# A gated linear-attention and bilinear-GLU kernel: another seven-product scheme for gate/up and q, seven products for 17 of 18 output row pairs, and an instruction order taken from a list scheduler inside the program

## The chip, the cores and the metric

The kernel runs on one core of one Trainium2 chip. The metric is the device time of one execution in microseconds (us), smaller is better. The kernel before took 592.59 us, the median of three runs (590.53 to 592.73).

## The reference, cut to what matters

`x` is 2048 x 512. Two branches read it and are mixed by a gate of each token:

```
qkv = x @ wqkv                       # 512 -> 3*512, 32 heads of 16
pq, pk = phi(q), phi(k)              # phi(t) = (t > 0 ? t + 1 : exp(t)) + 1e-6
kv = einsum("bhsd,bhse->bhde", pk, v);  z = sum_s pk
a  = (pq @ kv) / (pq @ z + 1e-6) @ wo
b  = ((x @ w_gate) * (x @ w_up)) @ w_down      # F = 1792
g  = sigmoid(sum(x * gate_w))
out = g * a + (1 - g) * b
```

Everything is float32. The kernel writes each factor as a rounded high part plus a rest and makes each product with three matmuls: high by high, high by low, low by high.

## The kernel before, in words

**First phase** (source lines 212 to 388). For 16 token tiles TensorE makes k = x wk (12 matmuls, `k_mm`) and adds phi(k)^T x to four accumulators (12 matmuls, `g_unit`). Beside it ScalarE and VectorE split the operands, and from step 6 on (`plan`) they prepare the sums of x blocks and of weights for the second phase.

**Second phase, units.** The tokens are halved into two `pair`s of 2 x 512 tokens. In each pair 14 column blocks of gate and up (`f`) and 2 of q (`q`) are made by 16 **units**, 32 in all (`unit`, L493). A unit is a 2 x 2 block product by seven products instead of eight; each product is 2 x 3 = 6 matmuls of 128 x 512 into one of four PSUM banks Y, X, R, S. Between products, ScalarE and VectorE move or add banks (`m2`, `t`, `cross`), and at the end VectorE multiplies gate by up.

**Weights of a unit.** Seven sums of weight blocks stand in a buffer `wr` (two buffers). `w_load` (L166) brings three blocks in one DMA on SyncE's queue; `w_add` (L173) makes two ScalarE copies and one accumulating DMA of 640 KB on GpSimd's queue; `w_high` and `w_low` split the seven sums into `wch` and `wcl` (two buffers each).

**Second phase, output jobs.** The outputs are sums over 18 rows of weights per pair (14 of w_down, 4 of the attention's folded `wp`), taken two rows at a time: nine row pairs per pair of tokens, 18 in all. Six of the 18 are **plain**: eight jobs (one for each 128 x 512 block of output) of two rows x 3 matmuls (`down_jobs`, L739), into `pdn`. Twelve go by **seven products** (`seven`, L792): seven steps, each of 2 x 3 matmuls for a row pair, two row pairs to a group, accumulated in `sa` and `sb`. Their operands are sums of `cross` tiles (split into `xh`, `xl`) and sums of weight rows (`ws`, split into `wh`, `wl`).

**Order.** Nothing is reordered behind the program's back: every engine runs its instructions in the order in which the code emits them. Which job goes between which products of a unit stands in the tables `FIRST` and `SECOND`, when a group opens in `FIRST_AT` and `STARTS`, and how far ahead ScalarE, VectorE and the loads may work in `LEAD_X`, `LEAD_W`, `MOST` and others (lines 32 to 59). The last thing computed is a plain row pair.

Helpers record most instructions, so the profile's lines are those of helpers: L79 matmul, L85 ScalarE, L88 and L91 VectorE, L109 a DMA from SyncE, L112 an accumulating DMA from GpSimd.

Of the kernel before, what the change touches and what calls it, by code (L numbers as in the profile page):

```python
# [14 lines left out]
P = 128  # L15
S = 2048
# [15 lines left out]
LEAD_X = 4  # L32
LEAD_W = 17
GAP_L = 6
GAP_A = 14
HB = 8
FIRST_SEVEN = (((4, 5), (6, 7)), (('a', 0), (8, 9)))
FIRST_AT = (4, 8)
MINUS_AT = (1, 2, 3)
XAT = (11, 6, 4, 8, 11, 7, 11, 13, 13, 13, 10, 13)  # L40
WUNIT = (8, 5, 2)
FIRST = (
    (3, 1, 3, 0), (0, 3, 2, 1), (0, 0, 1, 1), (2, 0, 1, 0), (0, 1, 0, 2), (0, 0, 0, 1), (1, 2, 0, 2), (0, 3, 0, 0),
    (0, 0, 2, 2), (0, 2, 3, 1), (2, 1, 1, 1), (3, 2, 0, 2), (2, 0, 1, 0), (3, 3, 3, 3), (1, 2, 0, 0), (3, 0, 2, 3),
)
PLACES = "high low e m c d t s r end".split()
ATT = ((0, 8, 5, 4, 6, 4, 5, 3), (0, 5, 12, 5, 0, 9, 4, 13))
NS = 58
SECOND = (
    (2, 1, 1, 0), (0, 0, 1, 3), (2, 1, 0, 3), (1, 0, 0, 0), (0, 1, 0, 2), (0, 0, 1, 2), (2, 0, 0, 2), (0, 2, 0, 1),  # L50
    (0, 2, 1, 2), (2, 2, 2, 0), (0, 0, 2, 1), (0, 3, 3, 1), (0, 3, 1, 0), (2, 2, 0, 1), (3, 0, 2, 3), (3, 1, 0, 2),
)
STARTS = (0, 4, 4, 10)
MOST = (2, 2, 2, 2)
MOST_0 = (1, 1, 2, 2)
LEAD_X0 = 4
LEADS_0 = (15, 7, 12)
RELOAD = ((0, 1), (0, 2), (3, 4), (5, 6))
Q_AFTER = ((5, 9), (0, 3))

SLOT = {3: 0, 4: 1, 2: 2, 5: 3, 1: 4, 6: 5, 7: 6}
# [3 lines left out]
def gated_mix(ctx: ExitStack, tc, xt, xp, x, wqkv, wq, wq_add, wo, wgu, wgu_add, wdn, gate_w, out):  # L71
# [39 lines left out]
    def dma_add(dst, src):  # L111
# [17 lines left out]
    own = {i: [const.tile([P, 2, CH], F32R, name=f"xc{i}{v}") for v in "hl"] for i in (1, 4, 6)}  # L129
    xc = {2: [v[:, 0:2] for v in xa], 7: [v[:, 2:4] for v in xa],  # L130
          3: [v[:, 0:2] for v in xb], 5: [v[:, 2:4] for v in xb], **own}


    zeros = own[1][0][:, 0, 0:CH // 2].bitcast(mybir.dt.bfloat16)
# [9 lines left out]
    xsum = {i: dram.tile([P, 2, CH], F32, name=f"xsum{i}") for i in (1, 5, 6, 7)}  # L144
# [28 lines left out]
    def w_add(n):  # L173

        if n < len(order):
            _, kind, m = order[n]
# [4 lines left out]
    PARTS = ((0, 2), (2, 4), (4, 7))  # L181
# [7 lines left out]
    def w_low(n, part):  # L189
        if n < len(order):  # L190
# [5 lines left out]
    SUMS = {1: (A1, B2, 0), 3: (B1, B2, 1), 4: (A2, A1, 1), 6: (A1, B1, 0), 7: (A2, B2, 0), 2: (None, A1, 0),  # L196
            5: (None, B2, 0)}

    def x_load(tile_, pair, i, ks):
        dma(tile_, xp[pair, SUMS[i][1]][:, ks])  # L200

    def x_add(tile_, pair, i, ks):
        one, _, sub = SUMS[i]
        if sub:
            act(tile_, tile_, scale=-1.0)
        if one is not None:
            dma_add(tile_, xp[pair, one][:, ks])
# [4 lines left out]
    with tc.tile_pool(name="p1", bufs=2, reuse_waits="tile") as p1:  # L212
# [127 lines left out]
        def cb_load(i):  # L340
            cbs[i] = p1.tile([P, 2, CH], F32, tag="cbs", name="cbs", bufs=3)
            x_load(cbs[i], 0, i, slice(0, 2))

        for t, i in zip((6, 7, 9, 10, 12), (4, 1, 6, 7, 3)):
            plan(t, lambda i=i: cb_load(i))
            plan(t + 2, lambda i=i: x_add(cbs[i], 0, i, slice(0, 2)))
            plan(t + 5, lambda i=i: split(*xc[i], cbs.pop(i)))
        for n, t in ((0, 8), (1, 11)):
            plan(t, lambda n=n: w_load(n))
            plan(t + 2, lambda n=n: w_add(n))  # L350
        plan(14, lambda: w_high(0))
        for part in range(3):
            plan(14 + part // 2, lambda part=part: w_low(0, part))
        plan(16, lambda: w_load(2))
# [36 lines left out]
    p2 = ctx.enter_context(tc.tile_pool(name="p2", bufs=1, reuse_waits="tile"))  # L391
    live = []
    spare, kept = [], {}

    class Buf:

        def __init__(self, name, rounded=False):
            self.home = rounded and bool(spare)
            one = spare.pop(0) if self.home else p2.tile([P, CH], F32R if rounded else F32, tag="s", name=name, bufs=NS)
            self.f = one.bitcast(F32) if rounded else one  # L400
            self.r = one
            if not self.home:
                live.append(self)
                assert len(live) <= NS, clock[0]

    def put(*some):
        for one in some:
            if one.home:
                spare.append(one.r)
            else:  # L410
                live.remove(one)

    def two(name):
        return [Buf(name + v, True) for v in "hl"]

    def split_buf(name, src, copy="act"):

        hi, lo = two(name)
        split(hi.r, lo.r, src, copy)
        return hi, lo  # L420


    at = {}

    def later(n, place, fn):
        at.setdefault((n, place), []).append(fn)

    def do(n, place):
        for fn in at.pop((n, place), []):
            fn()  # L430
        clock[0] += 1
        most = MOST if n >= units else MOST_0
        advance(dve=most[0], act=most[1])


    jobs, clock = [], [0]

    class Job:

        def __init__(self, mms, chains=(), after=None, apart=0, group=None, first=False):  # L440
            self.first, self.mms, self.after, self.apart, self.group = first, mms, after, apart, group
            self.chains = [list(c) for c in chains]
            self.free = [0] * len(self.chains)

    def always():
        return True

    def advance(**most):

        for i, job in enumerate(jobs):  # L450
            for k, chain in enumerate(job.chains):
                while chain:
                    kind, lead, gap, fn, ready = chain[0]
                    if lead < i or clock[0] < job.free[k] or not ready() or not most.get(kind, 1):
                        break
                    if kind in most:
                        most[kind] -= 1
                    fn()
                    job.free[k] = clock[0] + gap
                    chain.pop(0)  # L460

    owed, passed, running = [0], [0, 0], [None]

    def down(k, all_=False):

        owed[0] += k
        for _ in range(owed[0]):
            if not jobs or passed[0] - passed[1] < jobs[0].apart and not all_:
                break
            waits = [stage for chain in jobs[0].chains for stage in chain]  # L470
            if waits and not all_:
                break
            for kind, lead, gap, fn, ready in waits:
                assert ready(), clock
                fn()
            job = jobs.pop(0)
            running[0] = job.group
            owed[0] -= 1
            clock[0] += 1
            job.mms()  # L480
            passed[1] = passed[0]
            most = MOST_0 if job.first else MOST
            advance(dve=most[2], act=most[3])
            if job.after:
                job.after()
        if not jobs:
            owed[0] = 0


    def share(n):  # L490
        return SECOND[n - units] if n >= units else FIRST[n]

    def unit(n, quad=None, sign=None, og=None):  # L493

        wh, wl = wcs.pop(n)
        bank = {t: psum.tile([P, CH], F32, tag=t, name=f"b{t}") for t in "YXRS"}

        def reload(i):
            if n + 1 == units and i not in xsum:
                spare.extend(v[:, k] for v in xc[i] for k in range(2))  # L500
            elif n + 1 == units:
                hi, lo = xc[i]
                dma(lo.bitcast(F32), xsum[i])

                def high():
                    act(hi, lo.bitcast(F32))

                def low():
                    tt(lo, lo.bitcast(F32), hi.bitcast(F32), ALU.subtract)

                places, use = RELOAD[(1, 5, 6, 7).index(i)], {1: "d", 5: "t", 6: "s", 7: "r"}[i]
                assert places[0] <= places[1] <= PLACES.index(use)
                for fn, at_ in zip((high, low), places):
                    m, one = divmod(at_, len(PLACES))
                    later(units + m, PLACES[one], fn)

        def product(i, to, start=False):
            for k in range(2):
                ks = slice(k * P, (k + 1) * P)
# [25 lines left out]
        if n:  # L545
            w_high(n + 1)
# [4 lines left out]
        if n:  # L551
            w_low(n + 1, 0)
# [694 lines left out]
```

## Time and profile before

| | us |
|---|---|
| median of three runs | 592.59 |
| lowest, highest | 590.53, 592.73 |
| span of the profiled execution | 591.5 |
| TensorE (PE) busy | 583.7 |
| TensorE weight loads (PEld) busy | 478.0 |
| VectorE (DVE) busy | 491.3 |
| ScalarE (ACT) busy | 364.9 |
| GpSimd (POOL) busy | 100.3 |

The span runs from the first to the last instruction of one profiled execution. No whole time is listed for that execution; its span lies 1.1 us under the median of the runs. In the profile an arrow `out<-in` names the tile written and the tiles read. PE is a matmul, PEld its weight load (it runs beside the matmul before). A matmul's shown duration is longer than the distance to the next one, since matmuls are pipelined; so distances between starts are read, not durations.

### The profile page before, as it was taken

The numbers are of one execution on the slowest core, as the hardware profiler recorded it, in microseconds if no ns is written. First come the engines' busy times: TensorE is split into PE (matmuls) and PEld (weight loads), VectorE is DVE, ScalarE is ACT, GpSimd is POOL, SyncE is SP. The second block draws the span as 40 slices with busy tenths as digits, with TensorE's granted clock in tenths as the row PEclk, the third lists the DMA queues.
The fourth block names the chain that finished last, engine by engine and source line by source line (L and its number), as shares of the span: only waits on it lengthen the run. The fifth ranks groups of instructions, "written<-read, shape, count | busy, mean of one in ns | idle before, by whom it ended". The sixth has DMA issues, their size and how long they took to land.

```text
span 591.5 us, 7915 instructions
## 1 busy us (share of the span) xinstructions
PE 583.7 (99%) x2610; PEld 478.0 (81%) x2610; DVE 491.3 (83%) x798; ACT 364.9 (62%) x649; POOL 100.3 (17%) x123
## 2 busy tenths in 40 slices
PE   9999999999999999999999999999999999999997
PEld 6888888888888868788888788888888888888886
DVE  6877895775567889999869967998798999799987
ACT  3856774677647475688456747458956846646520
POOL 0011100000151124111020042305010322301000
PEclk9999999999999999999999999999999999999999
DMA  9476946868898879556798699779875676834003
GB/s 296 168 201 129 284 106 197 213 194 225 252 225 205 204 211 208 146 120 161 213 239 248 211 221 224 226 155 244 215 168 133 176 148 148 186 71 63 0 2 142
DMA packets 68249, 106.19 MB, mean 180 GB/s; under 512 B 8864, under 2 KB 40352, under 8 KB 68192
## 3 DMA queue, kind: packets, MB, share of 16 engines
q1 hardware_dynamic: 51872, 68.98, 35.5%
q0 software_dynamic: 16048, 36.18, 34.9%
q10 hardware_dynamic: 288, 0.52, 0.3%
q8 instruction: 20, 0.33, 0.2%
q14 instruction: 21, 0.17, 0.1%
HBM read 90.70 MB, written 15.61 MB: 180 GB/s over the span
## 4 chain that ended last, share of the span: by engine, by line
PE 90%; DVE 5%; issue 2%; DMA 2%; ACT 1%; POOL 0%; DVEq 0%; POOLq 0%; ACTq 0%
PE bY L79 13%; PE bX L79 13%; PE bR L79 13%; PE sa L79 11%; PE pdn L79 9%; PE sb L79 8%; PE pk L79 8%; PE gt L79 7%; PE bS L79 7%; DMA wr<-in_wgu_add 2%; DVE wcl L88 1%; DVE acc L88 1%; PE warm L79 1%; PE pw L79 0%; DVE cross L88 0%
## 5 line engine op out<-in xcount | busy, mean ns | idle before, releaser
L88 DVE TENSOR_TENSOR wcl<-wr,wch 128x512 fp32r<-128x512 f32 (+1 forms) x96 | 73.2, 772 | 2.0 <-ACT wch L85 1.9
L85 ACT ACTIVATE wch<-wr 128x512 fp32r<-128x512 f32 (+1 forms) x96 | 60.3, 691 | 4.9 <-DMA wr<-in_wgu_add 4.6
L112 POOL DMA_DIRECT2D wr<-in_wgu_add x28 | 25.0, 892 | 207.7 <-ACT wr L85 153.4
L79 PE MATMUL bX<-xbh,wch 128*128 128x512 f32 x128 | 47.3, 390 | 0.0
L79 PE MATMUL bX<-xbl,wch 128*128 128x512 f32 x128 | 47.2, 389 | 0.0
L79 PE MATMUL bX<-xbh,wcl 128*128 128x512 f32 x112 | 43.6, 389 | 0.0
L85 ACT ACTIVATE cross<-bY 128x512 f32<-128x512 f32 x32 | 19.0, 594 | 33.4 <-PE bY L79 33.3
L88 DVE TENSOR_TENSOR bR<-bX,m 128x512 f32<-128x512 f32 x32 | 22.2, 695 | 20.5 <-PE bX L79 19.6
L85 ACT ACTIVATE m<-bY 128x512 f32<-128x512 f32 x32 | 19.0, 593 | 31.7 <-PE bY L79 31.7
L112 POOL DMA_DIRECT2D ws<-dminus x27 | 31.1, 1341 | 35.7 <-DVE wl L88 24.7
L85 ACT ACTIVATE wr<-wr 128x512 f32<-128x512 f32 x64 | 36.4, 618 | 0.3 <-DMA wr<-in_wgu 0.3
L85 ACT ACTIVATE xh<-cross 128x512 fp32r<-128x512 f32 x38 | 23.5, 626 | 20.7 <-DVE cross L88 19.7
L88 DVE TENSOR_TENSOR t<-bR,cross 128x512 f32<-128x512 f32 x32 | 22.0, 687 | 15.0 <-PE bR L79 6.9
L88 DVE TENSOR_TENSOR acc<-pdn,acc 128x512 f32<-128x512 f32 (+1 forms) x39 | 25.4, 671 | 8.1 <-PE pdn L79 7.9
L85 ACT ACTIVATE cross<-bX 128x512 f32<-128x512 f32 x32 | 19.0, 593 | 21.3 <-DVE bS L88 21.2
L79 PEld LDWEIGHTS bX<-xbh,wch 128*128 128x128 f32 x128 | 24.0, 188 | 5.3 <-ACT cross L85 0.3
L79 PEld LDWEIGHTS bX<-xbl,wch 128*128 128x128 f32 x128 | 24.0, 188 | 5.0
L88 DVE TENSOR_TENSOR xl<-cross,xh 128x512 fp32r<-128x512 f32 x38 | 25.9, 684 | 2.4 <-ACT xh L85 2.2
L79 PE MATMUL bS<-xah,wch 128*128 128x512 f32 x64 | 25.1, 392 | 0.7 <-DVE bS L88 0.7
L112 POOL DMA_DIRECT2D ws<-in_wdn x18 | 24.1, 1721 | 9.1 <-DMA ws<-in_wdn 9.1
L79 PE MATMUL pdn<-hl,dh 128*128 128x512 f32 (+1 forms) x65 | 25.2, 388 | 0.0
L79 PE MATMUL pdn<-hh,dl 128*128 128x512 f32 (+1 forms) x65 | 25.1, 386 | 0.0
(310 smaller groups left out, 1823.6 us busy)
## 6 DMA issues: line engine op xcount, KB each, us to landing
wr<-in_wgu_add POOLq DMA_DIRECT2D x28, 640.0 KB, 6.9
wr<-in_wgu SPq DMA_DIRECT2D x28, 384.0 KB
ws<-in_wdn SPq DMA_DIRECT2D x45, 128.0 KB
xraw<-in_x SPq DMA_DIRECT2D x16, 256.0 KB
terms<-zq SPq DMA_DIRECT2D x16, 256.0 KB
zt<-terms SPq DMA_DIRECT2D x16, 256.0 KB
rb<-den SPq DMA_DIRECT2D x16, 256.0 KB
ws<-dminus POOLq DMA_DIRECT2D x27, 128.0 KB, 4.8
```

The lines of the kernel that those rows point to most:

```text
L79: tc.keep_in_program_order(nc.tensor.matmul(*args, **kw))
L85: pin(nc.scalar.activation(dst, src, func, **kw))
L88: pin(nc.vector.tensor_tensor(dst, a, b, op=op))
L112: tc.keep_in_program_order(nc.gpsimd.dma_start(dst, src, accum_op=ALU.add))
```

## The change

The program's second phase is written anew. In the new source the helpers are L72 and L532 (matmul), L78 and L503 (ScalarE), L510 (VectorE), L521 (DMA from SyncE) and L105 and L525 (accumulating DMA from GpSimd).

1. **Units.** Still seven products of six matmuls, but with other sums of x and of weights. The weight sums are a chain: each new block is the one before, copied or negated, plus a block added by DMA. `w_add` becomes three ScalarE copies and three accumulating DMAs (128, 128 and 256 KB) that wait for one another. Sums of results move partly into PSUM accumulation: VectorE has four whole-tile operations of a unit where it had five, ScalarE three as before.
2. **Output row pairs.** Seven products for 17 of the 18 row pairs; only pair 0's rows (0, 1) stay plain. The groups hold up to three row pairs, the last one four, and that last group ends the program. A weight sum of a step is reused: four accumulating DMAs for a row pair instead of five, five plain loads instead of six.
3. **Order.** All work of the second phase is first listed as operations with their readers and writers (`Op`). `plan` and `run` play them through with costs for each engine and DMA, and the instructions are emitted in the order of that play. TensorE takes the next product of a unit unless it is behind the table `SHARE` on output jobs.
4. **First phase.** Its own matmuls stay; the preparation of x sums and of the first two units' weights goes by the new chains, at steps given by `X_AT`, `W_AT` and `SPLIT_AT`.
5. The outputs of pair 0 leave on SyncE's queue instead of GpSimd's. Loads, splits, copies and stores that the changed sums need are added or dropped with them.

```diff
-FIRST_SEVEN = (((4, 5), (6, 7)), (('a', 0), (8, 9)))
...
-FIRST = (
-    (3, 1, 3, 0), (0, 3, 2, 1), (0, 0, 1, 1), (2, 0, 1, 0), (0, 1, 0, 2), (0, 0, 0, 1), (1, 2, 0, 2), (0, 3, 0, 0),
...
+LINE = (
+    (0, ((0, 1),)),
+    (0, ((2, 3), (4, 5), (6, 7))),
+    (0, (('a', 0), (8, 9), (10, 11))),
+    (0, ((12, 13), ('a', 1))),
+    (1, ((0, 1), (2, 3))),
+    (1, (('a', 0), (4, 5), (6, 7))),
+    (1, (('a', 1), (8, 9), (10, 11), (12, 13))),
+)
+SHARE = (0.0, 3.0, 6.8, 10.6, 14.5, 21.4, 29.5, 37.5, 45.6, 53.6, 61.6, 69.7, 77.7, 85.8, 93.8, 104.8, 129.0)
...
-            act(raws[n][:, 3:5], raws[n][:, 0:1].to_broadcast([P, 2, 2 * P]))
-            act(raws[n][:, 5:7], raws[n][:, 0:2], scale=-1.0)
-            dma_add(raws[n][:, 2:7], (wgu_add if kind == "f" else wq_add)[m])
...
+                act(raw[:, 3:4], raw[:, 2:3])
+                dma_add(raw[:, 3:4], more[:, 0:1], 0.72)
+                act(raw[:, 4:5], raw[:, 3:4], scale=-1.0)
+                dma_add(raw[:, 4:5], more[:, 1:2], 0.72)
+                act(raw[:, 5:7], raw[:, 4:5].to_broadcast([P, 2, 2 * P]))
+                dma_add(raw[:, 5:7], more[:, 2:4], 1.41)
...
+            product(1, "Y", True)
+            act(bk["R"], bk["Y"])
+            product(5, "X", True)
+            m5 = Buf("m5")
+            act(m5.f, bk["X"])
+            product(6, "R")
+            tt(bk["S"], bk["R"], m5.f, ALU.add)
+            product(2, "Y")
+            act(cross[0].f, bk["Y"], scale=-1.0 if turned[0] else 1.0)
...
+            product(7, "R")
...
+            product(3, "S")
...
+            product(4, "R")
...
+            def choose(engine, t):
...
+                if engine == "PE":
+                    some = [heads[s][at[s]] for s in "uj" if at[s] < len(heads[s])]
+                    if len(some) == 2 and at["j"] < share(at["u"]):
+                        some.reverse()
+                    for op in some:
+                        if open_[op] and may(op, t):
+                            return take(op, t)
+                    return
+                for op in sorted(ready[engine], key=lambda op: (late[op], op.id)):
+                    if may(op, t):
+                        return take(op, t)
```

Two places show what stands on an engine's list. On ScalarE, in the second of the units, where `wr` is the weight buffer, `wch` its rounded part, `m2` and `cross` copies of banks Y and X, `hh` the rounded h and `minus` a negated weight row, the list before reads:

```order
L85 ACTIVATE wch_1200<-wr_930 128x512
L85 ACTIVATE wch_1200<-wr_930 128x512 [waits DMASW7_49,Activation_49]
L85 ACTIVATE wch_1200<-wr_930 128x768 [waits Activation_49]
L85 ACTIVATE wr_1118<-wr_1118 128x512 [waits DMAHW6_49]
L85 ACTIVATE wr_1118<-wr_1118 128x512
L85 ACTIVATE minus_1217<-wdr_1007 128x256
L85 ACTIVATE cross1_1150<-bX_1121 128x512 [waits DVE_49]
L85 ACTIVATE hh_1239<-cross1_1150 128x512 [waits DVE_49]
L85 ACTIVATE m2_1257<-bY_1253 128x512 [waits PE_49]
```

The same place after, where `bR` is now written from `bY`, `m5` from `bX`, and `pws` and `woh` belong to the attention's weights:

```order
L503 ACTIVATE bR_1203<-bY_1177 128x512 [waits DVE_49,PE_49]
L503 ACTIVATE wr_1120<-wr_1120 128x256 [waits DMAHW3_49,Activation_49]
L503 ACTIVATE wch_1175<-wr_930 128x512
L503 ACTIVATE m5_1216<-bX_1195 128x512 [waits PE_49]
L503 ACTIVATE wch_1175<-wr_930 128x512 [waits DMASW4_49]
L503 ACTIVATE woh_1235<-wo_sb_1131 128x512 [waits DMAHW4_49]
L503 ACTIVATE pws_1238<-pw_1212 128x512 [waits PE_49]
L503 ACTIVATE cross0_1250<-bY_1177 128x512 [waits PE_49]
L503 ACTIVATE wr_1120<-wr_1120 128x256 [waits DMASW5_49]
L503 ACTIVATE minus_1254<-pws_1192 128x256 [waits Activation_49]
L503 ACTIVATE wr_1248<-wr_1248 128x256 [waits DMAHW1_49,DVE_49]
L503 ACTIVATE wch_1279<-wr_1120 128x768 [waits PE_49]
```

Copies of weights that wait for an accumulating DMA (`DMASW`) now stand between the copies of banks, and the buffers `wr_930`, `wr_1120` and `wr_1248` of three units are in work at once. On VectorE, at the end of the program, `acc` and `u2` are output blocks, `og` the gate, and `xc4` the reused space of a split `h`; the list before ends:

```order
L88 TENSOR_TENSOR cross0_5551<-bS_5506,cross0_5551 128x512 [waits PE_49]
L88 TENSOR_TENSOR cross0_5551<-cross0_5551,og_4991 128x512 [waits DVE_49]
L88 TENSOR_TENSOR xc4h_75<-cross0_5551,xc4h_75 128x512 [waits Activation_49]
L88 TENSOR_TENSOR acc_4482<-pdn_5619,acc_4482 128x512 [waits PE_49]
L88 TENSOR_TENSOR acc_4482<-acc_4482,og_4993 128x512 [waits DVE_49]
```

Eleven more rows follow there (eight sums from `pdn`, three gatings). After, 53 instructions of VectorE follow the last unit's last product (the row `cross0_5431<-bR_5364`); these stand at their end, ahead of the last three:

```order
L510 TENSOR_TENSOR xah_69<-cross1_5208,xah_69 128x512 [waits Activation_49]
L510 TENSOR_TENSOR xbl_72<-cross1_5429,xbh_71 128x512 [waits Activation_49]
L510 TENSOR_TENSOR u2_4181<-u2_4181,og_1060 128x512 [waits DVE_49]
L510 TENSOR_TENSOR u2_4186<-u2_4186,og_1060 128x512 [waits DVE_49]
L510 TENSOR_TENSOR acc_4474<-sb_5405,acc_4474 128x512 [waits PE_49]
L510 TENSOR_TENSOR acc_4479<-sb_5408,acc_4479 128x512 [waits PE_49]
L510 TENSOR_TENSOR acc_4474<-acc_4474,og_1056 128x512 [waits DVE_49]
L510 TENSOR_TENSOR acc_4479<-acc_4479,og_1056 128x512 [waits DVE_49]
L510 TENSOR_TENSOR acc_4576<-sa_5199,acc_4576 128x512 [waits PE_49]
L510 TENSOR_TENSOR acc_4584<-sa_5200,acc_4584 128x256 [waits PE_49]
L510 TENSOR_TENSOR acc_4584<-sa_5200,acc_4584 128x256
```

Splits of operands (`xah`, `xbl`) and gating of outputs, which stood ahead of the last matmuls or were few, now share VectorE's list with the last sums; three gatings come behind these.

More of the change, by code (lines that the diff above doesn't have):

```diff
@@ L406, in put @@
[L406 to L433, printed above, removed]
@@ L436, in gated_mix @@
[L436 to L460, printed above, removed]
@@ L462, in gated_mix @@
[L462 to L487, printed above, removed]
@@ L724, in gated_mix @@
[L724 to L745 removed]
+            dve("tensor_tensor", kv.f.rearrange("p (b e) -> p b e", b=KT)[sl, :, sl],
+                (pkv[sl, :, sl], bm[sl, None, sl].to_broadcast([P // 2, KT, P // 2])), 2 * P, op=ALU.mult)
@@ L1143, in plain @@
-    def plain(n):
-        return order[n][1] == "f" and (order[n][0], order[n][2]) not in row_of
-    ffn = [n for n in range(len(order)) if plain(n)]
-    def d_load(i):
-        if i < len(ffn):
-            n = ffn[i]
-            wdr[n] = Buf("wdr")
-            dma(wdr[n].f, wdn[order[n][2]])
-    d_load(0)
-    wp_load()
-    g_evac()
-    d_load(1)
-    rows = []
-    for some, place in SEVEN:
-        later(units + place, "end", lambda some=some: jobs.extend(
-            seven(1, [fps[1, key] for key in some], some == SEVEN[-1][0])))
@@ L1195, in gated_mix @@
-    down(len(jobs), True)
+                    tags.reverse()
+                    pd = bank(tags[0], "pdn")
+                    some = []
+                    for r in range(2):
+                        some += mm3(pd[:, cols], [v.r[:, sl] for v in one["rows"][r]],
+                                    [v.r[:, cols] for v in one["b"][r, c]], r == 0, r == 1, late=1)
+                    pe("j", some)
+                    to_acc(pair, i, pd, cols, o + step == CH)
+        STEPS = (1, 6, 2, 7, 5, 4, 3)
@@ L1198 @@
+        for pair, some in LINE:
+            if len(some) == 1:
+                plain(pair, some[0])
+            else:
+                seven(pair, some)
+        plan(todo_ops, units)
+    mix()
 def kernel(A_x, A_wqkv, A_wo, B_x, B_w_gate, B_w_up, B_w_down, gate_w):
```

1421 lines of the change are left out of this document (782 added, 639 removed).

## The prediction

> **What bounds the kernel now.** I read the page first, then clock and span, the chain of waits in order of time, TensorE's own waits, and stretches of the second phase.
>
> ```profile
> span 591.5 us, 7915 instructions
> ...
> PE 583.7 (99%) x2610; PEld 478.0 (81%) x2610; DVE 491.3 (83%) x798; ACT 364.9 (62%) x649; POOL 100.3 (17%) x123
> ...
> PE 90%; DVE 5%; issue 2%; DMA 2%; ACT 1%; POOL 0%; DVEq 0%; POOLq 0%; ACTq 0%
> ```
>
> ```profile
> core 0: 591.5 us, clock 0.999
> ```
>
> TensorE is busy nearly all the time, and the chain that ended last lies on it. The granted clock is full, so no clock gate plays a part. How dense the matmuls stand is read from pieces of the chain:
>
> ```profile
> 79.42 13.60 PE gt L79 x60
> 93.03 1.36 PE bY L79 x6
> ...
> 576.80 11.02 PE pdn L79 x54
> ```
>
> 13.60 / 60 is 0.2267 us from one 128 x 512 matmul to the next; six take 1.36 us. That is the price of a matmul here, not its shown duration. The last piece ends at 587.8, 3.7 us before the span does. TensorE's waits in all:
>
> ```profile
> PE warm L79 <- DVE xc1h L135: 1.3, 1, 1.3
> PE sb L79 <- ACT xh L85: 1.1, 1, 1.1
> PE sa L79 <- ACT xh L85: 0.7, 1, 0.7
> PE bS L79 <- DVE bS L88: 0.7, 1, 0.7
> PE sb L79 <- DVE xl L88: 0.2, 1, 0.2
> ```
>
> After the start only 2.7 us are lost. So TensorE's own work is the bound, and an edit can win by taking matmuls out, and lose by any new wait. Where the other engines stand, by stretches (columns: TensorE, weight loads, VectorE, ScalarE, GpSimd busy, clock, DMA share):
>
> ```profile
> 93.03:200.00 106.97, 106.97 (x527) 88.50 (x527) 71.16 (x112) 70.29 (x129) 18.94 (x22) 1.00 0.85 221
> 200.00:300.00 100.00, 97.99 (x425) 78.68 (x424) 91.53 (x148) 65.55 (x119) 17.59 (x20) 1.00 0.75 179
> ...
> 500.00:576.80 76.80, 76.80 (x340) 63.59 (x339) 68.43 (x109) 41.08 (x74) 11.42 (x13) 1.00 0.33 64
> ```
>
> VectorE is the next engine; DMA is fullest (0.85) in the first units.
>
> **The matmuls taken out.** Twelve row pairs by seven products become 17. A plain pair is 8 jobs x 6 = 48 matmuls, a seven-product one 7 x 6 = 42. Five pairs save 30, and 30 x 0.2267 = 6.8 us. (Of the program's last block two halves are cut in both; the count of whole matmuls falls by 27, of half ones by 6, the same work.) Units keep 42 matmuls. All of this lies on the path. The rows above leave no doubt that a matmul less is 0.2267 us less, as long as nothing else comes late: 60 of them follow each other with no gap.
>
> **VectorE and ScalarE.** A unit has four whole-tile VectorE operations where it had five. In all VectorE has about 20 instructions fewer and ScalarE some 78 more, most of them quarter-size copies of weights. What one costs in its engine's time is the distance between starts:
>
> ```profile
> 535.31 0.68 DVE L88 TENSOR_TENSOR wcl<-wr,wch 128x512 fp32r<-128x512 f32 x1
> 535.91 0.68 DVE L88 TENSOR_TENSOR xl<-cross,xh 128x512 fp32r<-128x512 f32 x1
> 536.51 0.68 DVE L88 TENSOR_TENSOR cross<-cross,cross 128x512 f32<-128x512 f32 x1
> ...
> 585.57 2.69 DVE L88 TENSOR_TENSOR acc<-pdn,acc 128x512 f32<-128x512 f32 x5
> ```
>
> 0.60 us. VectorE so loses some 12 us of work beside TensorE's matmuls: nothing on the path. If its cover goes, it is in the end, next.
>
> **The end of the program.** Before, the last unit's last product ends at 576.8 and 54 matmuls of a plain pair follow, with VectorE waiting for them; its last row (585.57 + 2.69) ends at 588.3, 0.4 us behind TensorE, and 3.2 us of output DMA follow. After, by the order of instructions, 135 matmuls follow the last unit's last product (129 whole, 6 half: 132 x 0.2267 = 29.9 us), and VectorE still has that product's multiplication, 49 whole and 4 half operations: 50 x 0.60 + 4 x 0.35 = 31.4 us (0.35 for a half is an estimate), begun about 0.3 us late: 31.7. So VectorE, not TensorE, closes the program, 1.8 us behind TensorE's work, plus 3.2 of DMA: 5.0 us against 3.7. That is +1.3 us if VectorE never waits. It will wait a little, since it takes each split from ScalarE and each sum from TensorE. I take +2.0. Bounds: +0.4 (only one more gating behind the last matmul; the rest hidden) and +5 (six waits of 0.6 us, one operation each).
>
> **Chained weight sums.** Per unit, one accumulating DMA of 640 KB becomes three that wait for each other. What such DMAs take from issue to landing:
>
> ```profile
> wr<-in_wgu_add POOLq DMA_DIRECT2D x28, 640.0 KB, 6.9
> ws<-dminus POOLq DMA_DIRECT2D x27, 128.0 KB, 4.8
> cbs<-in_xp POOLq DMA_DIRECT2D x5, 512.0 KB, 7.7
> cb<-in_xp POOLq DMA_DIRECT2D x10, 256.0 KB, 6.4
> ws<-in_wdn POOLq DMA_DIRECT2D x18, 128.0 KB, 6.6
> out<-acc POOLq DMA_DIRECT2D x8, 256.0 KB, 4.1
> ```
>
> A fifth of the bytes still takes two thirds of the time, so the chain is 4.8 + 4.8 + 6.4 = 16.0 us against 6.9. [...] Around the chain stand ScalarE's copies and the split:
>
> ```profile
> L88 DVE TENSOR_TENSOR wcl<-wr,wch 128x512 fp32r<-128x512 f32 x64 | 43.5, 683 | 2.0 <-ACT wch L85 1.9
> L85 ACT ACTIVATE wch<-wr 128x512 fp32r<-128x512 f32 x64 | 36.8, 620 | 4.9 <-DMA wr<-in_wgu_add 4.6 <-DMA wr<-in_wq_add 0.3
> L85 ACT ACTIVATE wr<-wr 128x512 f32<-128x512 f32 x64 | 36.4, 618 | 0.3 <-DMA wr<-in_wgu 0.3
> ```
>
> Three copies and the split are 3 x 0.62 + 0.62 + 0.68 = 3.2 us. The first load's landing isn't shown; between 4.1 and 6.9 (plain 256 KB, accumulated 640 KB) I take 5.5. One buffer is thus held 5.5 + 16.0 + 3.2 = 24.7 us; there are two, so 12.3 us a unit. TensorE's work of a unit is 42 x 0.2267 = 9.5 us plus output jobs of 1.36: by the order 10.2 to 12.2 us in the first eight units (mean 11.6) and 15.0 later. So the chain is even with TensorE at first and free afterwards, and it starts about one unit ahead: 8 x (12.3 - 11.6) = 6 us of lag fit into that lead of about 10 us. I cost it at nothing.
>
> What it also does: ScalarE, in order, now stops at three accumulating DMAs of a unit instead of one, and behind each stop stand the copies of banks for which TensorE waits. Before, it cost this:
>
> ```profile
> ACT wch L85 <- DMA wr<-in_wgu_add: 4.6, 2, 3.9
> ```
>
> ```profile
> 196.71 9.68 DMA wr<-in_wgu_add
> ```
>
> One late add (9.7 us) ran through ScalarE and VectorE to TensorE's wait of 1.1 + 0.2 us; the other two waits (0.7 each) were small queueing. The new order loses those places and gets its own. I take as much as before, 2.7 us, so no change. Bounds: none at all (-2.7), and a wait like that one for each of three times as many adds, 3 x 1.3 + 1.4 = 5.3 (+2.6).
>
> **First phase.** Weights of unit 0 are added one step (24 matmuls, 5.4 us) apart, and the first of these adds lies behind a 512 KB one (7.7 us), so ScalarE may stop for some 3 us there. It has this spare:
>
> ```profile
> ACT xnh L85 <- issue: 15.5, 8, 2.7
> ```
>
> It waits for TensorE by up to 2.7 us a step, and its splits are made a step ahead of use. Nothing; if the cover is gone, 2 us once. Pair 0's output DMAs on SyncE's queue instead of GpSimd's: nothing, the loads behind them are listed up to a unit ahead; if a load does come late by an output's 4.1 us, it costs part of that once.
>
> **The sum.** 591.5 - 6.8 + 2.0 + 0 = 586.7 for the span, plus 1.1 between the span and the median of the runs: 587.8.
>
> **The rivals.** *The gain is eaten by small waits:* VectorE's closing stretch at its bound (+5) and TensorE's waits at theirs (+2.6): 591.5 - 6.8 + 5 + 2.6 + 1.1 = 593.4. For it: VectorE is at 91.53 of 100 us in one stretch already, and the end asks more of it than it has. Against: it is freed of some 12 us of work earlier.
>
> *Slower: the weight chain bounds the first units.* If a 128 KB add takes the 6.6 us of the other row instead of 4.8, a buffer is held 24.7 + 2 x 1.8 = 28.3, a unit takes 14.1, and eight units lag 8 x (14.1 - 11.6) = 20 us, of which the lead hides 10. This gives 587.8 + 10 = 597.8, or up to 608 with no lead. It turns slower than no change from about 6.3 us an add. For it: that row, and the DMA share of 0.85 just there. Against: the rows of 6.6 are often two adds issued together, of which the second waits for the first, and the new program moves fewer bytes for each unit. One step apart from it, that the matmuls don't fall, is excluded: the count is in the list.
>
> **How the numbers follow.** The forecast has 0.60, small waits 0.23, the chain 0.17. About 0.5% (3 us) is what a measurement of this kernel can tell from no change: 589.6 to 595.6. Of the forecast's case 0.02 lies above 589.6, so faster 0.58, same 0.25, slower 0.17. The range: lowest with no waits and the smallest end, 587.8 - 2.7 - 1.6 = 583.5; half a microsecond more for the rounding of the pieces gives 583. Upward it takes in the small waits and the chain's price with the lead, to 599. The forecast's own range is 583 to 591.
>
> **What would show it.** Right: the same pitch of 0.2267 us, some 30 matmuls fewer in `sa`, `sb` and `pdn` together, TensorE's last matmul about 5 us before the end of the span and VectorE without gaps in the last 30 us, PE waits of 2 to 4 us in sum. Small waits: many PE waits under 1 us on `sa`, `sb` and `bR`, in the last 30 us above all. The chain: PE waits on `bY`, `bX` or `bR` between 100 and 200 us, with ScalarE waiting for `wr<-in_wgu_add` in front. The forecast is wrong if TensorE's waits exceed 6 us, or if the end runs otherwise than counted.

## The result, and the profile after

| | before | after |
|---|---|---|
| median, us | 591.56 | 619.22 |
| lowest, highest, us | 590.5, 592.73 | 615.57, 622.17 |
| span of the profiled execution, us | 591.5 | 617.0 |

Four runs of each. The ratio is 1.047, with an interval of 1.043 to 1.051: slower by 4.7% where 587.8 us was forecast, and 20 us above the range.

The page of the kernel after, first the head, then the shares of the chain that ended last:

```profile
span 617.0 us, 8100 instructions
...
PE 586.3 (95%) x2577; PEld 474.1 (77%) x2577; DVE 468.7 (76%) x777; ACT 387.8 (63%) x727; POOL 155.7 (25%) x184
...
PE 41%; DMA 23%; issue 15%; ACT 9%; DVE 6%; POOL 4%; SPq 1%; POOLq 0%; DVEq 0%; ACTq 0%
```

The matmuls fell as counted (2610 to 2577, some of them half ones), but the chain that was 90% TensorE is now 41%. DMA has 23% of it and ScalarE 9%.

Where the time lies is read from the first unit's start and the last matmul's. TensorE's timeline, before and then after:

```profile
92.86 0.39 PE L79 MATMUL bY<-xah,wch 128*128 128x512 f32 x1
...
587.52 0.28 PE L79 MATMUL pdn<-xc4h,dh 128*128 128x256 f32 x1
```

```profile
92.65 0.39 PE L532 MATMUL bY<-xah,wch 128*128 128x512 f32 x1
...
610.57 0.28 PE L532 MATMUL sa<-xbl,xal 128*128 128x256 f32 x1
```

The first phase is the same to 0.2 us. From the first unit's start to the last matmul it was 494.7 us and is 517.9. With 6.8 us less to multiply, 23.2 + 6.8 = 30.0 us have been lost there. Behind the last matmul's start stood 4.0 us and now 6.4. So 591.5 - 0.2 - 6.8 + 30.0 + 2.4 = 616.9, the span of 617.0 up to rounding.

The second phase in stretches (columns as in the prediction), the kernel before's sum and then the kernel after:

```profile
sum 494.77, PE 492.07 PEld 404.01 DVE 416.46 ACT 307.30 POOL 92.97; mean PE 98.41 PEld 80.80 DVE 83.29 ACT 61.46 POOL 18.59
```

```profile
93.00:200.00 107.00, 100.45 (x484) 81.41 (x482) 54.28 (x81) 60.77 (x120) 25.43 (x30) 0.98 0.66 157
200.00:300.00 100.00, 95.31 (x410) 77.91 (x411) 82.20 (x138) 71.62 (x139) 35.23 (x41) 0.98 0.78 179
300.00:400.00 100.00, 95.86 (x409) 76.32 (x408) 84.76 (x136) 71.79 (x134) 30.06 (x35) 0.98 0.84 202
400.00:500.00 100.00, 95.75 (x414) 76.75 (x413) 80.73 (x132) 66.71 (x127) 33.39 (x39) 1.00 0.74 162
500.00:610.70 110.70, 107.11 (x473) 87.89 (x471) 91.33 (x152) 59.23 (x110) 21.08 (x24) 1.00 0.44 100
sum 517.70, PE 494.48 PEld 400.29 DVE 393.28 ACT 330.12 POOL 145.19; mean PE 98.90 PEld 80.06 DVE 78.66 ACT 66.02 POOL 29.04
```

TensorE stands idle 517.7 - 494.5 = 23.2 us where it was 2.7, spread over the whole phase, not only over its first units. The other 9.5 us are matmuls farther apart than 0.2267 us: the first ones after a wait (0.33 us behind the stall below), and some at half pace (last section). What TensorE waits for, in the kernel after (us in total, times, longest):

```profile
PE bR L532 <- ACT bR L503: 14.6, 9, 3.8
PE bR L532 <- DVE bS L510: 3.1, 4, 1.2
PE pkv L532 <- DMA wv<-in_wqkv: 2.2, 2, 1.6
PE sb L532 <- ACT sb L503: 1.7, 1, 1.7
```

The largest is the wait for the bank copy `bR<-bY` on ScalarE. And what ScalarE waits for:

```profile
ACT wr L503 <- DMA wr<-in_wgu_add: 65.1, 34, 6.0
ACT wr L503 <- DMA wr<-in_wgu: 27.3, 12, 5.3
```

Before, ScalarE waited 4.6 us for these adds (at `wch`) and 0.3 for these loads. One stall can be seen whole, ScalarE and then TensorE:

```profile
275.79 1.14 ACT L503 ACTIVATE wch<-wr 128x512 fp32r<-128x512 f32 x2
280.11 0.42 ACT L503 ACTIVATE wr<-wr 128x256 f32<-128x256 f32 x1 [3.18 <-DMA wr<-in_wgu_add]
280.43 0.58 ACT L503 ACTIVATE bR<-bY 128x512 f32<-128x512 f32 x1
```

```profile
274.14 0.39 PE L532 MATMUL bY<-xah,wcl 128*128 128x512 f32 x1
...
276.86 0.39 PE L532 MATMUL sa<-xl,wh 128*128 128x512 f32 x1
281.07 0.50 PE L532 MATMUL bR<-xc6h,wch 128*128 128x512 f32 x1 [3.82 <-ACT bR L503]
```

The last matmul into bank Y starts at 274.14. Its copy into bank R, ready to run from about 275, starts at 280.43, since ScalarE's next instruction is a weight copy that waits for an accumulating DMA until 280.11. TensorE stands still for 3.82 us behind it. Six of TensorE's nine waits for this copy are longer than 0.5 us. Ahead of four of them ScalarE had stopped at `wr` for 2.4 to 6.0 us, and ahead of one at `ws<-dminus` for 3.2 us. The sixth (3.05 us, at 362.77) is mostly queueing: ahead of it ScalarE worked through other instructions, with stops of only 0.6 and 0.8 us.

### The profile page after: what moved, and what is told of

It reads as the page before. It is cut to its first block, busy times and chain, and to the rows that moved or that the text cites. A ratio compares the mean times of both kernels' runs of the same rounds, so it can differ in the third digit from the quotient of the medians.

```text
span 617.0 us, 8100 instructions
## 1 busy us (share of the span) xinstructions
PE 586.3 (95%) x2577; PEld 474.1 (77%) x2577; DVE 468.7 (76%) x777; ACT 387.8 (63%) x727; POOL 155.7 (25%) x184
## 4 chain that ended last, share of the span: by engine, by line
PE 41%; DMA 23%; issue 15%; ACT 9%; DVE 6%; POOL 4%; SPq 1%; POOLq 0%; DVEq 0%; ACTq 0%
DMA wr<-in_wgu_add 11%; PE pk L72 7%; PE gt L72 7%; PE sa L532 7%; PE bR L532 7%; PE sb L532 6%; DMA wr<-in_wgu 4%; PE bY L532 4%; POOL ws L525 2%; PE bS L532 2%; POOL wr L525 2%; ACT wch L503 2%; DMA ws<-in_wdn 2%; PE bX L532 2%; DVE wcl L510 1%
## 5 line engine op out<-in xcount | busy, mean ns | idle before, releaser
L525 POOL DMA_DIRECT2D wr<-in_wgu_add x78 | 72.6, 934 | 233.0 <-ACT wr L503 197.6
L503 ACT ACTIVATE wr<-wr 128x256 f32<-128x256 f32 (+1 forms) x90 | 43.6, 486 | 97.5 <-DMA wr<-in_wgu_add 65.1
L510 DVE TENSOR_TENSOR wcl<-wr,wch 128x512 fp32r<-128x512 f32 (+1 forms) x93 | 70.5, 774 | 20.8 <-ACT wch L503 20.4
L503 ACT ACTIVATE wch<-wr 128x512 fp32r<-128x512 f32 (+1 forms) x93 | 62.4, 695 | 13.2 <-DMA wr<-in_wq_add 5.5
L532 PE MATMUL bY<-xah,wch 128*128 128x512 f32 x128 | 50.8, 397 | 0.0
L525 POOL DMA_DIRECT2D ws<-dminus x39 | 42.9, 1257 | 29.3 <-DVE wl L510 8.1
L532 PE MATMUL bY<-xah,wcl 128*128 128x512 f32 x112 | 44.5, 398 | 0.0
L532 PE MATMUL bR<-xc6h,wch 128*128 128x512 f32 x64 | 26.4, 412 | 14.7 <-ACT bR L503 14.6
L503 ACT ACTIVATE xh<-cross 128x512 fp32r<-128x512 f32 x46 | 28.6, 624 | 10.7 <-DVE cross L510 10.7
L510 DVE TENSOR_TENSOR xl<-cross,xh 128x512 fp32r<-128x512 f32 x39 | 26.5, 685 | 7.4 <-ACT xh L503 7.4
L532 PE MATMUL bY<-xal,wch 128*128 128x512 f32 x80 | 31.6, 395 | 0.0
L510 DVE TENSOR_TENSOR bS<-bR,m 128x512 f32<-128x512 f32 x32 | 22.2, 693 | 11.1 <-PE bR L532 6.1
L532 PEld LDWEIGHTS bR<-xc6h,wch 128*128 128x128 f32 x64 | 12.0, 187 | 22.1 <-ACT bR L503 19.8
L532 PE MATMUL bR<-xc7h,wch 128*128 128x512 f32 x64 | 26.0, 406 | 3.1 <-DVE bS L510 3.1
L532 PEld LDWEIGHTS bY<-xah,wch 128*128 128x128 f32 x128 | 24.5, 191 | 5.2
L503 ACT ACTIVATE cross<-bY 128x512 f32<-128x512 f32 x32 | 18.9, 589 | 11.7 <-PE bY L532 11.4
L532 PE MATMUL bR<-xbh,wch 128*128 128x512 f32 x64 | 25.2, 393 | 0.6 <-DVE cross L510 0.6
L532 PE MATMUL bR<-xc6h,wcl 128*128 128x512 f32 x64 | 25.3, 395 | 0.0
L532 PEld LDWEIGHTS bY<-xah,wcl 128*128 128x128 f32 x112 | 21.6, 193 | 4.6
L532 PE MATMUL bR<-xc6l,wch 128*128 128x512 f32 x64 | 25.1, 393 | 0.0
L510 DVE TENSOR_TENSOR cross<-bR,cross 128x512 f32<-128x512 f32 x28 | 19.2, 684 | 7.9 <-PE bR L532 7.1
L532 PE MATMUL bR<-xc7l,wch 128*128 128x512 f32 x64 | 25.1, 392 | 0.0
```

What stands on the lines that cost most here:

```text
L503: return Op("ACT", lambda: pin(nc.scalar.activation(get(dst), get(src), func, **{k: get(v) for k, v in kw.items()})), c, c + 0.11, [src, * ...
L510: return Op("DVE", lambda: pin(getattr(nc.vector, name)(get(dst), *[get(v) for v in ins], **kw)), c, c + 0.085, some, [dst], kind="dve")
L525: return Op("POOL", lambda: pin(nc.gpsimd.dma_start(get(dst), get(src), accum_op=ALU.add)), 0.54, 0.0, [src, dst], [dst], work=work, kind= ...
L532: tc.keep_in_program_order(nc.tensor.matmul(get(dst), get(lhs), get(rhs), **kw))
```

## The experiments

**Theory S:** ScalarE, in order, is made to stop at DMAs that the play which sets the order believed landed, and the bank copies stand behind the stop. **Rivals:** the new unit itself leaves too little room between a bank's last matmul and its reuse (B); the chain is simply too long or the DMA engines too full (C); any reshuffling moves the time by some 20 us (N). The play counts a DMA as landed a fixed time after its transfer, 0.82 us on SyncE's queue and 1.42 us on GpSimd's. What a run adds to these times is called reserve here. All medians in us; the kernel before in the same runs had 591.2 to 592.2.

| run | chain of adds | landings in the play | median | ratio to before, interval | ScalarE waits for `wr` loads and adds | TensorE waits after the start |
|---|---|---|---|---|---|---|
| before | | | 591.4 | | 5.2 | 2.7 |
| after | yes | as written | 619.2 | 1.047 [1.043, 1.051] | 112.6 | 23.0 |
| e10 | yes | +0.75 us | 599.6 | 1.013 [1.008, 1.019] | 65.8 | 10.4 |
| e3 | yes | +1.5 | 590.8 | 0.998 [0.996, 1.000] | 34.9 | 5.1 |
| e7 | yes | +3.0 | 618.1 | 1.045 [1.042, 1.049] | 13.3 | 18.8 |
| e5 | yes | +1.5, adds only | 594.6 | 1.005 [1.003, 1.007] | 49.2 | 6.9 |
| e6 | yes | +1.5, loads only | 603.1 | 1.017 [1.013, 1.021] | 93.3 | 13.7 |
| e4 | copies on GpSimd | as written | 625.9 | 1.058 [1.055, 1.060] | 45.7 | 30.3 |
| e13 | copies on GpSimd | +1.5 | 598.4 | 1.010 [1.007, 1.014] | 31.1 | 10.6 |
| e1 | no sums | as written | 602.0 | 1.018 [1.012, 1.024] | 0 | 9.7 |
| e11 | no sums | +1.5 | 583.3 | 0.988 [0.984, 0.991] | 0 | 0.9 |
| e2 | sums on VectorE | as written | 594.9 | 1.007 [1.004, 1.010] | 0 | 9.2 |
| e8 | sums on VectorE | +1.5 | 585.8 | 0.990 [0.989, 0.992] | 0 | 2.6 |
| e9 | sums on VectorE | +3.0 | 582.3 | 0.985 [0.983, 0.987] | 0 | 1.1 |
| e12 | e8, plain end | +1.5 | 583.6 | 0.987 [0.985, 0.989] | 0 | 1.2 |
| e14 | e9, plain end | +3.0 | 584.0 | 0.987 [0.985, 0.989] | 0 | 1.4 |

The last two columns add up the rows of the views of waits of each profiled execution.

**e1, without the chain.** One 896 KB load of all seven blocks, no copies, no adds. The sums of weights are left out, so the output isn't the reference's:

```diff
-dma(wr_nodes[n][:, 0:3], (wgu if kind == "f" else wq)[m], 1.18)
+dma(wr_nodes[n][:, 0:7], (wgu if kind == "f" else wq)[m], 2.75)
...
-act(raw[:, 3:4], raw[:, 2:3])
-dma_add(raw[:, 3:4], more[:, 0:1], 0.72)
...
```

> The seven weight blocks of a unit come in one plain load of 896 KB; the sums of weight blocks are left out (so the products are not the reference's), with them the three accumulating DMAs of a unit and ScalarE's three copies. Same matmuls, order played anew. Theory S (ScalarE, in order, stops at the copies that wait for chained accumulating DMAs, and the bank copies behind them come late for TensorE): no such stops, TensorE's waits on bR under 4 us in sum, 584 to 594 us. Rival B (the new units leave too short a distance between a bank's copy and its next use, so that any queueing on ScalarE or VectorE is a wait): waits on bR stay over 10 us, 608 us or more.

**e2, the sums on VectorE.** One 512 KB load and four VectorE sums in place of copies and adds:

```diff
+tt(raw[:, 3:4], raw[:, 3:4], raw[:, 2:3], ALU.add)
+tt(raw[:, 4:5], raw[:, 0:1], raw[:, 3:4], ALU.subtract)
+tt(raw[:, 5:6], raw[:, 4:5], raw[:, 2:3], ALU.add)
+tt(raw[:, 6:7], raw[:, 4:5], raw[:, 1:2], ALU.add)
```

> The whole result is computed. Four weight blocks come in one plain load of 512 KB and VectorE makes the four sums (128 x 256 each, about 0.35 us), so some 1.4 us more VectorE work a unit, 45 us in all; no accumulating DMA for unit weights. Theory S: TensorE's waits on bR fall under 6 us, 586 to 598 us, VectorE about 510 us busy. Rival B: 612 us or more, and worse than without the chain alone because VectorE is fuller.

**e3, reserve in the play.** The instructions are the same in number (2577, 777, 727, 184 on the four engines); only the landing times in the play's model differ, and so the order:

```diff
-IN, OUT, PART = {"SP": 1.07, "POOL": 1.42}, {"SP": 0.82, "POOL": 1.42}, ...
+IN, OUT, PART = {"SP": 1.07, "POOL": 1.42}, {"SP": 2.32, "POOL": 2.92}, ...
```

> Only the play's landing times are changed: each DMA is played 1.5 us later at landing, so that readers are listed later. Theory S with the cause in landings that come later than played: ScalarE's waits for wr<-in_wgu_add fall from 65 us to under 35, time 596 to 608 us. If the stops come from something the play doesn't have at all (late loads in bursts), 612 to 622 us. Rival B: unchanged, 616 to 622 us.

**e4, the chain's copies on GpSimd.** The three `act` of a unit's chain in the second phase become GpSimd instructions.

> The chain of three accumulating DMAs stays in the second phase, but its three copies are made by GpSimd instead of ScalarE; ScalarE waits for the chain only at the split. Theory S: ScalarE's waits for wr vanish, TensorE's waits on bR fall to under 7 us, 590 to 604 us; the accumulating DMAs of the output weights, which queue behind these copies on GpSimd, may come late and cost part. If the chain's mere length is the cost (weights late, not ScalarE stopped): 615 us or more, with TensorE waiting for wch or wcl. Rival B: 612 us or more with waits on bR.

These four: e1 came to 602.0, above S's 584 to 594 and below B's 608, with waits on `bR` of 8.0 us, between the two as well. e2, 594.9, is as S said. e3, 590.8, is better than S's 596 to 608: a pair of numbers in the model is worth 28.4 us. ScalarE's waits in e3:

```profile
ACT wr L503 <- DMA wr<-in_wgu_add: 10.3, 12, 2.6
ACT wch L503 <- DMA wr<-in_wgu_add: 8.3, 7, 1.7
...
ACT wr L503 <- DMA wr<-in_wgu: 4.7, 4, 2.1
```

65.1 and 27.3 have become 10.3 and 4.7 us, and TensorE's wait for the copy `bR<-bY` 0.7 us instead of 14.6. Unit, chain and DMA bytes are the same, and the adds landed no sooner (medians of 4.3 us for 128 KB and 5.6 for 256 KB, against 4.1 and 4.3), so neither B nor C can be the whole. But e4 missed by far (625.9 against 590 to 604): off ScalarE, the chain lost more. Its waits:

```profile
ACT wh L503 <- DMA ws<-dminus: 24.2, 5, 7.8
...
ACT wch L503 <- DMA wr<-in_wgu_add: 20.3, 13, 3.5
ACT wch L503 <- DMA wr<-in_wq_add: 17.8, 5, 5.7
```

ScalarE now stops at the splits of the same weights and at those of `ws`. Freed of the copies it is still an in-order engine behind late DMAs. And the copies themselves came later than played. The run's page has:

```profile
L517 POOL TENSOR_SCALAR wr<-wr 128x256 f32<-128x256 f32 (+1 forms) x90 | 118.0, 1313 | 197.8 <-DMA wr<-in_wgu_add 127.4
```

That is 1.31 us a copy by the mean (spans on GpSimd are rough), where this run's play was given 0.65 for each of a unit's two copies of 128x256 and 1.15 for the one of 128x512, 0.82 by the mean: about 1.5 us more for the three copies of a unit. So e4 also brought in a cost that the play had too low. That made the theory one about the play's belief, whichever instruction then stops. Four runs on this:

**e5, e6, e7.** The same line as in e3, with 2.92 for GpSimd's adds alone, with 2.32 for SyncE's DMAs alone, and with both 3.0 longer.

> The changed kernel, but in the play that sets the order the landing of GpSimd's accumulating DMAs alone is 1.5 us longer (1.42 to 2.92); that of SyncE's loads stays at 0.82. Theory S (ScalarE, in order, is made to stop at DMAs that the play believed landed, and bank copies stand behind the stop): of the 92 us in which ScalarE waited for weights in the changed kernel, 65 were for the accumulating DMAs, so most of the gain of the run with both landings longer (619.2 to 590.8) comes here: 592 to 602, with ScalarE's wait for wr<-in_wgu_add under 25 us and its wait for the plain load wr<-in_wgu still there, 15 us or more. Rival L (the loads at the head of the chain are what is late, and the adds behind them inherit it): 605 to 619. Rival N (any reshuffling of the order moves the time by some 20 us, with no rule in it): anywhere, and ScalarE's waits do not follow what was lengthened.

> The other half: in the play only SyncE's loads land 1.5 us later (0.82 to 2.32), the accumulating DMAs as in the changed kernel. Theory S: 607 to 616, with ScalarE's wait for the plain load wr<-in_wgu gone (under 8 us of 27) and its wait for the adds still 45 us or more. Rival L: 590 to 600. Rival N: no relation between what was lengthened and which wait goes.

> Both landings 3.0 us longer in the play instead of 1.5. Theory S: ScalarE's waits for weights shrink further (from about 19 us to under 8), but TensorE's waits were already small, so the time stays within 3 us of the run with 1.5 (588 to 594). It would rise again only if the play, believing transfers slow, holds TensorE back for them. Rival N: a new order, so some value between 590 and 620 with TensorE's waits of 10 us or more.

e5 and e6 show that the wait which goes is that of the DMA which was lengthened. In e5 the wait of `wr` for the adds is 17.5 us (of 65.1) and that for the loads 12.6 (of 27.3), not the 15 or more expected. In e6 the wait for the loads is gone from the list and that for the adds 58.0; at the split `wch` the wait for the adds even grew, from 2.4 to 17.2. e6's time (603.1) is 4 us better than expected. The two gains, 24.6 and 16.1 us, overlap; that a late load also delays its adds would explain this, and was not tested apart. N has no reason for which wait goes.

e7 refutes S as first put: ScalarE hardly waits for weights (13.3 us), and the time is 618.1. TensorE's waits in e7:

```profile
PE bR L532 <- ACT wch L503: 6.0, 6, 1.7
PE sb L532 <- ACT sb L503: 5.7, 2, 4.5
PE bX L532 <- ACT wch L503: 2.2, 3, 1.2
```

TensorE now waits for the splits `wch` and `wcl` (11.6 of its 18.8 us), which the order puts late. Its longest single wait, 4.5 us for `sb`, is of the old kind: ScalarE had stopped 3.3 us at `xsum<-cb` and 2.8 us at `terms<-zq` just ahead. In the play a buffer is held, by its own numbers, for load and adds 6.1 + 6.6 + 6.6 + 7.2 = 26.5 us and, with the 3.2 us of copies and split from the prediction, 29.7: 14.8 a unit for two buffers, above the 11.6 of TensorE. So by these numbers the play itself is bound by a chain that on the chip is 4.1 + 4.1 + 4.3 us of adds (the medians of the kernel after), and the order that it makes is built around waits that the chip doesn't have. With 1.5 the same sum gives 11.8, about even. The order suffers on either side of the truth. This was worked out after e7; e9 tests it.

**e8, e9.** Sums on VectorE as in e2, with the landings 1.5 and 3.0 longer. Without the chain the play has no such bound, so more reserve should not hurt: this parts S from N.

> The four weight sums on VectorE out of one 512 KB load (no accumulating DMA for them), and the landing in the play 1.5 us longer. This was 594.9 without the longer landing. Theory S: no chain and few stops: TensorE's waits on banks fall to 2 to 4 us in sum and the time to 586 to 592, with VectorE some 40 us fuller than in the changed kernel and the end of the program (VectorE behind TensorE by some 6 us) as it was. Rival B (the new unit leaves too little room between a bank's last matmul and its reuse, whatever stands behind DMAs): TensorE's waits on banks stay at 6 us or more and the time at 593 to 598.

> Weight sums on VectorE (no chain) and landings 3.0 us longer in the play. With the chain, 3.0 gave 618.1 us where 1.5 gave 590.8. Theory S, second part: in the play with 3.0 the chain of load and three adds holds a weight buffer so long that the play itself makes TensorE wait for it (its own count of TensorE's idle time is 49 us, against 6 with 1.5), and the real engines then work off an order made around waits that do not exist. Without the chain the play holds no such wait (5.3 us idle with 3.0 too), so the time stays where it was with 1.5 (585.8): 584 to 589. Rival N (any other order scatters between 586 and 620): a value off by 5 us or more, most likely 592 to 615.

585.8 lies at the lower end of what S expected of e8 (586 to 592), 582.3 is below what it expected of e9 (584 to 589), and the opposite of N. e9 has the lowest median of all runs. Its stretches:

```profile
200.00:300.00 100.00, 100.00 (x443) 82.80 (x442) 93.51 (x172) 69.21 (x128) 17.60 (x20) 1.00 0.76 204
300.00:400.00 100.00, 100.00 (x443) 82.81 (x442) 99.41 (x171) 69.19 (x121) 14.12 (x16) 1.00 0.54 149
400.00:500.00 100.00, 100.00 (x443) 82.81 (x442) 96.21 (x175) 62.42 (x112) 10.55 (x12) 1.00 0.50 135
```

In them TensorE is without a gap, although VectorE is busy 99.41 of 100 us. Full is not late.

**e10, e11.** Reserve of 0.75 with the chain, and of 1.5 without sums.

> The chain as in the changed kernel, landings 0.75 us longer in the play. Theory S: between the run with none (619.2) and that with 1.5 (590.8), nearer to the latter since half of the stops by count are shorter than 1 us: 595 to 608, ScalarE's waits for weights between the two (40 to 60 us of 92 and 23). Rival N: no order in the values.

> All seven weight blocks loaded by one 896 KB DMA with the sums left out (as in the run without the chain, 602.0 us), and landings 1.5 us longer in the play. Theory S: that run's remaining 14 us were the same fault on the loads (ScalarE stopped at the splits for them), so this one falls to 583 to 590 with TensorE's waits on banks under 4 us. Rival C (what the run without the chain lost was the DMA engines' load, 896 KB a unit instead of 384 and 512): 597 to 604, no change.

e10, 599.6, lies between as expected; its waits for weights are as expected too (40 to 60): 53.5 us in the rows that the expectation counts, those of `wr` and `wch` for `in_wgu` and `in_wgu_add` in the second phase (65.8 in the table, which counts all). e11, 583.3, is as S expected, and that the DMA engines are too full falls with it: seven raw blocks a unit cost nothing that can be seen once the order has reserve. So e1 missed by the same fault; there ScalarE had waited 14.8 us for `ws<-dminus` in place of `wr`. Like e1, e11 leaves the sums out.

**e12, e14.** The program's end on a plain row pair again:

```diff
-(1, (('a', 1), (8, 9), (10, 11), (12, 13))),
+(1, (('a', 1), (8, 9), (10, 11))),
+(1, ((12, 13),)),
```

> Weight sums on VectorE, landings 1.5 us longer in the play, and the program ends on a plain row pair as the kernel before did (the last group has three row pairs, rows 12 and 13 of pair 1 are plain): six matmuls more (1.4 us) for a shorter end. The end of the changed kernel lies 6.3 us behind the last matmul, that of the kernel before 3.7 us, and VectorE, closing the program, also makes TensorE wait in the last 30 us. If the end is worth what the step of the prediction on it said (+2.0), this gives 585.8 + 1.4 - 2.0 to 3 = 584 to 586; if VectorE's closing hides behind nothing else, 582 to 584; if the end costs nothing, 587.

> Weight sums on VectorE, landings 3.0 us longer in the play (582.3), and the plain row pair at the end: with 1.5 the plain end brought 2.1 us (585.8 to 583.6) for six matmuls more. If the two add up: 580 to 581.5. If the plain end had only removed waits that the longer landings remove as well: 582 to 584, since its six matmuls cost 1.4 us.

2.1 us better on e8, 1.7 us worse on e9, so e14 is as its second case had it. Behind the last matmul's start stand 5.6 us in e9 and 4.4 in e14: once the other waits are gone, the plain end saves no more than its six matmuls (1.4 us) cost.

**e13, copies on GpSimd, with reserve.**

> The chain kept with its copies on GpSimd, as in the run that came to 625.9 us against the expectation of 590 to 604, now with landings 1.5 us longer in the play. Theory S, as the runs since have shaped it (the fault is the play's belief about landings, whichever engine then stops): 584 to 593, with ScalarE's waits for weights under 20 us and TensorE's waits on banks under 5. Rival G (GpSimd's copies, some 0.5 us a block and more, lengthen the chain and occupy GpSimd's queue, so the chain itself is what is slow there): 605 to 626.

598.4 lies between the two expectations. Reserve took 27.5 us off e4, as it took 28.4 off the kernel after. For the 7.6 us by which e13 stays above e3, Rival G has its evidence in the trace: between 93 and 575 us GpSimd was busy 258.7 us with 256 instructions where e3 has 145.3 us with 168, about 1.3 us for each one more, with the copies still played as 0.65 and 1.15, and ScalarE waits 23.3 us for the adds at `wch` where e3 has 8.3. A run with these costs put right in the play was not made, so the share of each stays open.

In all four variants that were run both ways, 1.5 us of reserve shortened the time: by 28.4 us (as changed), 27.5 (copies on GpSimd), 18.8 (no sums) and 9.2 (sums on VectorE). N, by which the values have no order, can't account for that.

## Why the prediction was wrong

- **The step that failed:** "ScalarE, in order, now stops at three accumulating DMAs of a unit instead of one, and behind each stop stand the copies of banks for which TensorE waits. ... I take as much as before, 2.7 us, so no change", with an upper bound of 5.3. The mechanism was named, and its size was missed: TensorE's listed waits came to 23.0 us, and with the wider distances 30.0 us were lost. The bound took the one late add that had reached TensorE in the old order and counted it three times for the whole program. In the new order ScalarE stopped 34 times at `wr` for adds and 12 times for loads. The sum asked how many adds there are, not with how much reserve the order places what reads them. The source had the answer: an add of 128 KB is played, when nothing else moves, as 1.42 + 0.72 + 1.42 = 3.6 us, and the prediction's own row for such DMAs has 4.8 (after: 4.1); a unit's load is played as 1.07 + 1.18 + 0.82 = 3.1 us and took 3.6. Half of them come later than the median, and ScalarE's longest single wait for one was 6.0 us.
- **Matmuls taken out, -6.8:** right, as far as e9 can show it, where nothing else comes late. Its span of 581.1 us lies 10.4 us below the kernel before. From the first unit's start to the last matmul's it is 11.7 us shorter: 6.8 for the matmuls, and 4.9 that are about what the kernel before lost in its own waits (2.7 us, and the wider distances behind them). The end is 1.6 us longer, and the first unit starts 0.3 earlier.
- **The weight chain, nothing:** its length was not what lost the time; whether its own price is nothing stays open (below). Adds landed in 4.1, 4.1 and 4.3 us by the medians, 12.5 against the 16.0 taken. The chain was faster than taken, and the loss came all the same. (Two of its three copies are 128x256 and took 0.41 us each, not the 0.62 taken.) The rival on the chain (pivot at 6.3 us an add) is refuted also by place: of 23.2 idle us only 6.6 lie before 200 us. The sign that the prediction gave for it, waits on `bR` with ScalarE waiting for an add in front, did appear, but over the whole phase, so that sign doesn't tell the chain from late stops.
- **VectorE's 12 us beside TensorE, nothing:** right; VectorE's busy time fell by 23 us and bought nothing, and e8 and e9 gave it 40 more at no cost.
- **The end, +2.0:** right in size, in part by luck. The time behind the last matmul's start grew by 2.4 us. VectorE closes it at 612.9, which is 1.6 us more behind that start than before, near the 1.3 counted; the rest is the output DMA after it, 4.1 us where the prediction kept 3.2:

```profile
610.17 1.47 DVE L510 TENSOR_TENSOR acc<-sa,acc 128x512 f32<-128x512 f32 x3 [0.27 <-PE sa L532]
611.55 1.35 DVE L510 TENSOR_TENSOR acc<-acc,og 128x512 f32<-128x512 f32 x3
```

- **First phase, nothing:** right; the first unit starts 0.2 us earlier.

The forecast's condition ("wrong if TensorE's waits exceed 6 us") is the one that was met. That the late stops are the cause is shown by e3, by the same step in the other three variants and, term by term, by e5 and e6. Not every wait is one: the 3.05 us at 362.77 are mostly queueing. How much of the 5.1 and 8.5 us between e3 and e8 or e9 belongs to the chain, and how much to ScalarE's copies for it, stays open.

## What to carry to other kernels

Where an order comes from a played model, hold each of its costs against the trace, and not only against the median: an in-order engine that stops for a landing later than the play believed holds up everything queued behind it (in the stall shown above ScalarE stopped for 3.18 us, and TensorE stood still for 3.82). Reserve has an upper end too, where the modelled transfer becomes a bound of the play itself; here a shorter dependence (one load, and the sums on VectorE) took that end away at the reserve tried. Before costing a new wait from the old trace, ask what stands right behind it in the new order.

## What the runs showed of the hardware

After some of its waits of about 2 us or more TensorE fell to about half its pace for a few matmuls, and not always at once. Behind the stall shown above, in the kernel after:

```profile
281.63 0.40 PE L532 MATMUL bR<-xc6h,wcl 128*128 128x512 f32 x1
281.87 0.39 PE L532 MATMUL bR<-xc6h,wch 128*128 128x512 f32 x1
...
283.22 0.63 PE L532 MATMUL bY<-xal,wch 128*128 128x512 f32 x1
283.65 0.63 PE L532 MATMUL bY<-xah,wcl 128*128 128x512 f32 x1
284.07 0.63 PE L532 MATMUL bY<-xah,wch 128*128 128x512 f32 x1
```

The distance is 0.24 us at first and then 0.43, for about seven matmuls: 1.4 us on top of the wait of 3.82. The granted clock from 282.37 to 285.35 was 0.50, and 1.00 ahead of the wait. Take as a gap the distance between two starts less the usual 0.2267 us. From the first unit's start on, in before, after, e1, e2 and e4 together, all five gaps of 2.9 us or more (after 3.98 and 3.20, e1 2.92, e4 5.89 and 4.36) were followed by such a stretch of some five to eleven matmuls, at distances of 0.42 to 0.43 us. Four of ten gaps between 1.9 and 2.7 us were too (e1 2.45 and 2.17, e2 2.14, e4 2.32), and no shorter one. So in these runs gaps of about 2 us have been enough in four of ten cases.
